# Two steps of six Fourier transforms in 64-by-64 parts of the matmul array

## The chip, the cores and the metric

The kernel runs on one core of a Trainium2 chip. The metric is the device time of one execution in microseconds. TensorE (PE) multiplies matrices into PSUM, VectorE (DVE) and ScalarE (ACT) work on SBUF and PSUM, GpSimd (POOL) on SBUF; SyncE (SP) and ACT issue most of the DMAs.

## The reference

Two blocks follow each other. The first filters each of the 8 sequences of 3008 tokens and 256 channels in the frequency domain; the second is a gated feed-forward layer on the 24064 tokens that result.

```python
def _attn_ref(x, filt_r, filt_i):                 # x: (8, 3008, 256), float32
    X = np.fft.rfft(x, axis=1)
    F = (filt_r + 1j * filt_i)[None, :, :]        # (1505, 256)
    Y = X * F
    y = np.fft.irfft(Y, n=x.shape[1], axis=1)
    return y.astype(np.float32)

def _moe_ref(x, w_gate, w_val, w_out):            # d_ff = 1536
    g = x @ w_gate
    silu = g * (1.0 / (1.0 + np.exp(-g)))
    val = x @ w_val
    return (silu * val @ w_out).astype(np.float32)
```

## The kernel before

All arithmetic is float32. One sequence is one transform b, 0 to 7. Its length is 47 x 64 (N1 = 47, N2 = 64, token = 64 n1 + n2), and it is done in four steps, each a set of matmuls against tables made on the host:

- First step, tiles pa. For each of the 64 values of n2, a 47-point transform over n1, of which the half spectrum of NS = 24 frequencies s is kept. For transforms 2 to 7 this is `stage1_paired` (L633): five values of n2 at a time (NP), 13 units; `pair` (L626) first makes, on DVE, the sums and differences of the rows n1 and 47 - n1 (L259 and L256), so that the real part comes from the sums (L639) and the imaginary part from the differences (L641). Two products of 256 columns per unit, one ACT copy (L645), one DMA from ACT's queue into the array d1 in DRAM. Transform 1 uses `stage1` (L658), transform 0 a form of its own before the main loop.
- Middle step there, tiles pb: `stage2a`, L698. For each s, the twiddle factors and the 64-point transform over n2 as one 128x128 table (64 complex points are 128 real rows), read from later_tbl. Two frequencies form a unit, 12 units. DVE then multiplies by the filter: the real part for all rows (L707), the imaginary part for the two halves of the partitions exchanged (L711, with the negation, and L714), and POOL adds (L256).
- Middle step back, tiles pc: `stage2b`, L731, the inverse over n2 for the same frequencies; ACT copies (L739), and the result goes to d2 in DRAM.
- Last step, tiles pd: `stage3`, L765, the inverse over s back to 47 values of n1, giving chunks y of 8 x 47 tokens (halved as TQ = 188 columns) with channels on partitions.

The feed-forward layer works on four chunks k of each transform and three groups g of the hidden width: 12 steps per transform, run by class Group. It multiplies polynomials of the blocks in a form that saves products: products P, Q (into banks wk), A, B (banks wa), E (banks we), all at L862, with sums on DVE, ACT and POOL between them; the projection W to the output (banks wA, wF, wG, L959) and its sums o (L256). While transform b is in its 12 steps, the pieces of transform b + 1 are woven in: the list `plan` says which piece belongs to which step, and each piece is a Python generator, of which every `yield` ends one stage.

The order is written out by hand. SCHEDULE (L88) is one step as a list of tokens; a token such as Q1, s13 or g12 names one operation of the group, a mark ' one of the group before, t1.2 the third stage of the second piece of the plan. `pin` keeps every engine's instructions in this order. There are no engine priorities: each engine takes its instructions in order and waits for what it needs.

Eight PSUM banks of 512 columns exist. Seven form the pool wps, which the products of the feed-forward layer share; one is the pool fps, which the pieces pa, pb, pc and pd of transforms 1 to 7 use in turn (`bank`, L620; fbank). The SBUF area lent (L213) holds the tables, inputs and outputs of the middle step. At marked tokens of each step SP issues the reload of the next group's weights wt_t (`reload_weights`, L405).

Of the kernel before, what the change touches and what calls it, by code (L numbers as in the profile page):

```python
# [41 lines left out]
FP32 = mybir.dt.float32  # L42
# [16 lines left out]
NH = 4  # L59
# [13 lines left out]
NP = 5  # L73
NPAIR = N1 // 2
N_PAIRED = -(-N2 // NP)

# [12 lines left out]
Q0 o3' z1.o' t4.2' W2 f0 S00' S01' i0 x0.o' t0.0 x1.o' i1 Q1 t0.1 x2.o' P3 i2 x3.o' f1 t4.3' W1 i3  # L89
x4.o' S10' x03 S11' i4 s13 x5.o' P1 i5 o1 t0.2 P0 o2 i6 z0.o c1 i7 D01 A13 g1 c0 i8 S20' Q2 S21' g0  # L90
y01 m13 t1.0 h0 i9 f2 s01 W6 t1.1 h1 i10 x23 D02 P2 o6 D12 A01 i11 c2 B13 g2 n3' m01 t0.3 S30' t1.2
x02 W7 S31' g13 y12 y02 B01 h13 o7 t1.3 t2.0 s02 s12 g01 h2 Q3 t2.1 h01 e12 A02 y23 W4 e02 y03 m02
g3 A12 o4 z2.o t2.2 E12 m12 B02 t2.3 l12 E02 u12 e13 g02 t3.0 h3 s23 l02 B12 v12 E13 t3.1 h02 u02
A23 n2 l13 g12 v02 W5 s03 e23 h12 e01 m23 A03 o5 z3.o u13 E23 t3.2 m03 v13 E01 l23 e03 t3.3 t4.0 l01
u23 B23 v23 u01 t4.1 E03 n1 v01 g23 B03 l03 W3 h23 g03 u03 h03 v03
# [6 lines left out]
""".split()  # L102
BLOCKS = (0, 1, 3, 2)
# [21 lines left out]
def dft_tables():  # L125
# [30 lines left out]

    paired = np.zeros((NP * (NPAIR + 1), 2, NP, NS))
    for j in range(NP):
        paired[NPAIR * j:NPAIR * (j + 1), :, j] = w[1:NPAIR + 1]
        paired[NP * NPAIR + j, 0, j] = 1.0  # L160
    paired = paired.reshape(NP * (NPAIR + 1), -1)


    pairs = np.arange(128).reshape(2, N2).T.ravel()
    later = np.stack([de[:, :, 0], de[:, :, 1][:, :, pairs]], 2)
    f32 = np.float32
    return (wf.reshape(NR, NK).astype(f32), wi.reshape(NK, NR).astype(f32),
            back.astype(f32), paired.astype(f32), np.ascontiguousarray(de).astype(f32),
# [4 lines left out]
def kernel(  # L173
# [11 lines left out]
    wf_host, wi_host, back_host, paired_host, de_host, later_host = dft_tables()  # L185
    wf_dram = nc.inline_tensor(wf_host, name="wf_tbl")
    wi_dram = nc.inline_tensor(wi_host, name="wi_tbl")
    paired_dram = nc.inline_tensor(paired_host, name="paired_tbl")
# [34 lines left out]

    def weights_of(b, k, g):
        return wt_1 if b == 0 and k < NT and g == 1 else wt_t
# [6 lines left out]
    w_dram = wdpool.tile([NG, 128, NPR, 2, 128], FP32, name="w_all")  # L232
    wo_t = cpool.tile([128, NJ, 7, 128], FP32)
# [19 lines left out]
    pin = tc.keep_in_program_order  # L253

# [229 lines left out]
    back_t, paired_t, differences, third = [], [], [], []  # L484

    def load_back():

        for n in range(3):
            t = rpool.tile([128, 2, 128], U32, name=f"paired_{n}", tag="pw", bufs=3)
            t = t.bitcast(FP32).rearrange("p b f -> p (b f)")  # L490
            (differences if n else paired_t).append(t[0:NP * (NPAIR + (not n))])
        t = rpool.tile([128, 2, 128, 2], U32, name="x_third", tag="raw", bufs=2)
        t = t.bitcast(FP32).rearrange("p b f two -> p (b f two)")
        third.append(t[0:NP * (NPAIR + 1)].rearrange("p (i c) -> p i c", c=C))
        pin(nc.sync.dma_start(out=paired_t[0][:, 0:2 * NP * NS], in_=paired_dram.ap()))
        t = rpool.tile([128, 2, 128, 2], U32, name="back", tag="raw", bufs=2)
        t = t.bitcast(FP32).rearrange("p b f two -> p (b f two)")
        back_t.append(t[:, 0:10 * N1])
        pin(nc.sync.dma_start(out=back_t[0], in_=back_dram.ap()))
# [15 lines left out]
    class Spectral:  # L515
# [25 lines left out]
        def load_x(self, u):  # L541
            if self.b == 0:
                rows = x[0].rearrange("(r n) c -> r n c", n=32)
                for a, n in ((0, 4), (4, 4)):
                    for r in (slice(0, 80), slice(80, NR)):
                        self.load(out=x0[u][r, a:a + n, :],
                                  in_=rows[r, 8 * u + a:8 * u + a + n, :])
            elif self.b > 1:
                if u < N_PAIRED:
                    t = third[0]  # L550
                    if u % 3 < 2:
                        t = xpool.tile([NP * (NPAIR + 1), 2, C], FP32, name=f"x_{self.b}_{u}",
                                       tag="x")
                    n2, pairs = min(NP * u, N2 - NP), NP * NPAIR
                    rows = x[self.b].rearrange("(n1 n2) c -> n2 n1 c", n2=N2)
                    back = bass.AP(tensor=x.tensor,
                                   offset=x.offset + ((self.b * N1 + N1 - 1) * N2 + n2) * C,
                                   ap=[[C, NP], [-N2 * C, NPAIR], [1, C]])
                    self.load(out=t[0:pairs, 0], in_=rows[n2:n2 + NP, 1:NPAIR + 1])
                    self.load(out=t[0:pairs, 1], in_=back)  # L560
                    self.load(out=t[pairs:pairs + NP, 0], in_=rows[n2:n2 + NP, 0])
                    self.x[u] = t
            elif u < N_ONE:
                self.x[u] = xpool.tile([NR, NV, C], FP32, name=f"x_{self.b}_{u}", tag="x")
                rows = x[self.b].rearrange("(r n) c -> r n c", n=32)

                for r in (slice(0, 80), slice(80, NR)):
                    self.load(out=self.x[u][r], in_=rows[r, ts(u, NV), :])

        def load_two(self, u):  # L570
            if u < N_TWO:
# [10 lines left out]
                if self.b < 2:  # L582
                    self.load(out=self.t2[u], in_=self.twos(self.d1, u))
                    return
                rows = self.d1.rearrange("a n c -> (a n) c").rearrange(
                    "(n s p) c -> p n s c", n=N2, p=2)
                for i in range(2):
                    self.load(out=self.t2[u][N2 * i:N2 * (i + 1)], in_=rows[i, :, ts(u, NV)])
# [37 lines left out]
        def pair(self, u):  # L626

            if u < N_PAIRED:
                a, b = [self.x[u][0:NP * NPAIR, i] for i in range(2)]
                pin(sub(nc.vector, differences[u % 2], a, b))  # L630
                pin(add(nc.vector, a, a, b))

        def stage1_paired(self, u):  # L633

            t1 = t1pool.tile([NP * NS, 2, C], FP32, name=f"t1_{self.b}_{u}", tag="t1", bufs=2)
            ps = self.bank(f"pa_{self.b}_{u}")[0:NP * NS]
            table = paired_t[0]
            m = NP * NS
            pin(nc.tensor.matmul(out=ps[:, 0], lhsT=table[:, 0:m], rhs=self.x.pop(u)[:, 0],  # L639
                                 start=True, stop=True))  # L640
            pin(nc.tensor.matmul(out=ps[:, 1], lhsT=table[0:NP * NPAIR, m:2 * m],  # L641
                                 rhs=differences[u % 2], start=True, stop=True))
            self.load_x(u + 3)
            yield
            pin(nc.scalar.copy(out=t1, in_=ps))  # L645
            n2 = min(NP * u, N2 - NP)

            rows = self.d1.rearrange("a n c -> (a n) c").rearrange("(r p) c -> r (p c)", p=2)
            pin(nc.scalar.dma_start(out=rows[NS * n2:NS * (n2 + NP)],
                                    in_=t1.rearrange("p i c -> p (i c)")))  # L650
            yield
            self.pair(u + 2)
# [449 lines left out]
    older = before = None  # L1102
    pieces_before = []
# [52 lines left out]
    for b in range(B):  # L1156
# [8 lines left out]
        if b:  # L1165
            one = [nxt.stage1_paired(u) for u in range(N_PAIRED)] if nxt else []
        else:
            one = [nxt.stage1(u) for u in range(N_ONE)]
        two = []
        for u in range(N_TWO + 2) if nxt else ():  # L1170
            two += [nxt.stage2b(u - 2)] if u > 1 else []
            two += [nxt.stage2a(u)] if u < N_TWO else []
        if nxt:
            plan[0] = one[0:2] + d[0][0:1] + one[2:3] + d[0][1:2]
            plan[1] = one[3:4] + d[0][2:3] + one[4:5] + d[0][3:4] + one[5:6]
            plan[2], plan[3] = (one[6:10], one[10:13]) if b else (one[6:11], one[11:16])
            plan[4] = d[1] + two[0:1]

            plan[5], plan[6] = [iter(())] + two[1:5], two[5:10]
            plan[7] = two[10:11] + d[2]  # L1180
            plan[8], plan[9] = two[11:16], two[16:21]
            plan[10], plan[11] = two[21:24], three(nxt, 0)
# [10 lines left out]
        for step in range(NCHUNK * NG + (b == B - 1)):  # L1193
# [16 lines left out]
            for place, token in enumerate(SCHEDULE):  # L1210
# [8 lines left out]
                elif op[0] == "t":  # L1219
                    n = int(op[1])  # L1220
                    ps = pieces_before if old else pieces
                    if n < len(ps):
                        next(ps[n], None)
                elif op[0] in "Wo" or op.endswith(".o"):
# [10 lines left out]
                if nxt and (step, op) == ((4, "P2") if b else (5, "A23")):  # L1235
                    nxt.load_two(0)
                if b + 2 < B and (step, op) in ((10, "Q2"), (10, "B01"), (11, "Q2")):

                    following.load_x(2 if step == 11 else int(op == "B01"))
                if b + 2 < B and step == 11 and op in ("A02", "B02"):  # L1240
                    following.pair(int(op == "B02"))
# [43 lines left out]
```

## Time and profile before

| what | value |
|---|---|
| three timed runs | 2888.11, 2889.03 and 2891.69 us, median 2889.03 us |
| profiled execution | 2891.35 us, of which the trace spans 2889.6 us |
| mean granted clock of TensorE | 0.998 of full speed |
| DMA | 558.89 MB, mean 193 GB/s |

The profile's page gives for each engine its busy time and the count of its instructions. PE is a matmul, PEld the load of its stationary operand, which overlaps the matmuls. In a group's row the columns are: line, engine, operation, output and inputs, shape, count, then the busy time and the mean of one in ns, then the idle time of the engine before it with what ended it. A float32 product of the program is two MATMUL rows and two LDWEIGHTS rows in the trace.

### The profile page before, as it was taken

How to read it: one execution, taken by the hardware profiler on the slowest of the kernel's cores; microseconds unless marked ns; L12 is line 12 of the kernel's file. 1: busy time of each engine (PE TensorE's matmuls, PEld its weight loads, DVE VectorE, ACT ScalarE, POOL GpSimd, SP SyncE). 2: the span in 40 equal slices, each digit the busy share in tenths (PEclk: the TensorE clock that was granted, in tenths of full speed). 3: DMA queues.
4: the chain of work that ended last, by engine and by line, in shares of the span. 5: the costliest groups of instructions: out<-in, count | busy, mean ns of one | idle time of the engine just before them, and what ended most of it. 6: DMA issues, size and time to landing. Idle time of an engine off the chain costs nothing.

```text
span 2889.6 us, 47316 instructions
## 1 busy us (share of the span) xinstructions
PE 2843.4 (98%) x14784; PEld 2434.3 (84%) x14784; DVE 2075.8 (72%) x4663; ACT 1576.1 (55%) x4190; POOL 1534.5 (53%) x1671
## 2 busy tenths in 40 slices
PE   7999999999999999999999999999999999999998
PEld 5777878888888888888888888888888888888887
DVE  6898767776767766777767677677677767766666
ACT  6775445555555455555555554555555555555554
POOL 4885665555445554446453555444554544555453
PEclk9999999999999999999999999999999999999999
DMA  8677865666566765667656566566665666645443
GB/s 227 218 265 245 278 209 176 181 219 196 182 190 180 229 185 184 197 182 216 196 183 197 179 208 205 177 195 184 209 193 189 185 205 195 206 142 161 147 137 82
DMA packets 396367, 558.89 MB, mean 193 GB/s; under 512 B 201079, under 2 KB 296585, under 8 KB 396117
## 3 DMA queue, kind: packets, MB, share of 16 engines
q1 hardware_dynamic: 366533, 506.80, 57.5%
q10 hardware_dynamic: 27792, 45.72, 4.7%
q0 software_dynamic: 1792, 3.34, 0.4%
q8 instruction: 120, 1.97, 0.3%
q14 instruction: 130, 1.06, 0.1%
HBM read 460.38 MB, written 95.34 MB: 192 GB/s over the span
## 4 chain that ended last, share of the span: by engine, by line
PE 87%; POOL 3%; issue 1%; DVE 1%; DMA 0%; ACT 0%; POOLq 0%; SPq 0%; DVEq 0%
PE wa L862 23%; PE wA L959 15%; PE wk L862 15%; PE we L862 12%; PE wG L959 8%; PE wF L959 3%; PE pd L765 3%; PE pc L731 2%; PE pb L698 2%; PE pa L639 1%; PE pa L641 1%; POOL out_dram L944 1%; POOL h L259 1%; DMA lent<-later_tbl 0%; DVE o L256 0%
## 5 line engine op out<-in xcount | busy, mean ns | idle before, releaser
L862 PE MATMUL wa<-y_t,wt_t 128*128 128x188 f32 x4464 | 879.1, 323 | 7.9 <-DMA y_t<-yt 1.7
L862 PEld LDWEIGHTS wa<-y_t,wt_t 128*128 128x128 f32 x4464 | 748.8, 190 | 89.3 <-ACT wa L888 11.3
L256 POOL TENSOR_TENSOR h<-h 128x376 f32<-128x376 f32 x190 | 184.9, 994 | 776.4 <-DVE h L909 776.4
L259 POOL TENSOR_TENSOR h<-h 128x376 f32<-128x376 f32 x572 | 565.5, 1010 | 15.4 <-DVE h L256 15.2
L862 PEld LDWEIGHTS wk<-y,wt_t 128*128 128x128 f32 x2976 | 500.9, 190 | 80.2 <-ACT f L877 0.8
L862 PE MATMUL wk<-y,wt_t 128*128 128x188 f32 x2976 | 565.1, 323 | 0.0
L959 PE MATMUL wA<-h,wo_t 128*128 128x376 f32 x1532 | 549.0, 481 | 3.5 <-DVE o L256 3.2
L862 PE MATMUL we<-y_t,wt_t 128*128 128x188 f32 x2232 | 431.7, 323 | 0.8 <-ACT we L893 0.7
L259 DVE TENSOR_TENSOR we<-we,m 128x376 f32<-128x376 f32 x576 | 316.4, 554 | 134.8 <-PE we L862 86.8
L959 PEld LDWEIGHTS wA<-h,wo_t 128*128 128x128 f32 x1532 | 279.2, 190 | 109.0 <-issue 3.5
L862 PEld LDWEIGHTS we<-y_t,wt_t 128*128 128x128 f32 x2232 | 369.4, 190 | 1.6 <-ACT we L893 0.9
L259 POOL TENSOR_TENSOR D<-f,f 128x376 f32<-128x376 f32 x288 | 280.5, 986 | 131.9 <-ACT f L877 123.2
L897 ACT COPY m<-wa 128x376 f32<-128x376 f32 x576 | 271.7, 472 | 86.0 <-PE wa L862 82.8
L263 DVE SCALAR_TENSOR_TENSOR y<-wk,c 128x376 f32<-128x376 f32 x480 | 243.1, 539 | 82.4 <-ACT we L893 53.9
L904 ACT ACTIVATE u<-we 128x188 f32<-128x188 f32 x576 | 188.8, 328 | 191.0 <-DVE we L259 170.9
L959 PE MATMUL wG<-h,wo_t 128*128 128x376 f32 x768 | 274.0, 479 | 0.0
L904 ACT ACTIVATE g<-wa 128x188 f32<-128x188 f32 x576 | 187.2, 326 | 157.2 <-PE wa L862 143.9
L877 ACT ACTIVATE f<-wk 128x376 f32<-128x376 f32 x288 | 139.1, 483 | 224.5 <-PE wk L862 153.8
L881 ACT COPY c<-wk 128x376 f32<-128x376 f32 x288 | 136.0, 472 | 215.7 <-PE wk L862 215.7
L884 DVE SCALAR_TENSOR_TENSOR x<-wk,f 128x376 f32<-128x376 f32 x192 | 104.1, 542 | 199.3 <-PE wk L862 196.9
L893 ACT COPY we<-y 128x376 f32<-128x376 f32 x480 | 220.8, 479 | 39.4 <-DVE h L909 24.7
L909 DVE TENSOR_TENSOR h<-wa,g 128x188 f32<-128x188 f32 x576 | 196.2, 345 | 31.5 <-ACT g L904 30.6
(157 smaller groups left out, 3857.8 us busy)
## 6 DMA issues: line engine op xcount, KB each, us to landing
wt_t<-w_all SPq DMA_DIRECT2D x174, 896.0 KB
wt_t<-w_all SPq DMA_DIRECT2D x174, 768.0 KB
lent<-later_tbl SPq DMA_DIRECT2D x84, 256.0 KB
lent<-in_filt_r_dram SPq DMA_DIRECT2D x336, 64.0 KB
d<-lent ACTq DMA_DIRECT2D x84, 256.0 KB
d<-t ACTq DMA_DIRECT2D x78, 240.0 KB
lent<-d SPq DMA_DIRECT2D x144, 128.0 KB
t<-d SPq DMA_DIRECT2D x112, 128.0 KB
```

What stands on the lines that cost most here:

```text
L256: return eng.tensor_tensor(out=dst, in0=a, in1=b, op=ALU.add)
L259: return eng.tensor_tensor(out=dst, in0=a, in1=b, op=ALU.subtract)
L263: return nc.vector.scalar_tensor_tensor(out=dst, in0=a, scalar=-1.0, in1=b, op0=ALU.mult, op1=ALU.subtract)
L862: pin(nc.tensor.matmul(out=ps[:, z], lhsT=self.wt[:, SLOT[p], z], rhs=rhs, start=start and z == 0, stop=True, skip_group_check=True))
L877: pin(act.mul(self.small(f"f{i}", f"f{i}", 1), t[f"k{i}"], -1.0))
L881: pin(act.copy(out=self.small(f"c{i}", f"c{i}", 1), in_=t[f"k{i}"]))
L884: pin(v.scalar_tensor_tensor(out=dst, in0=t[f"k{j}"], scalar=-1.0, in1=t[f"f{i}" if j == 3 else f"D{at}"], op0=ALU.mult, op1=ALU.add))
L893: pin(act.copy(out=self.bank(f"e{at}"), in_=t[f"y{at}"]))
L897: pin(act.copy(out=self.small(f"m{at}", "m", 4), in_=t[f"a{at}"]))
L904: pin(act.activation(out=self.small(op, "g", 3, 1)[:, 0], in_=ps[:, 1], func=AF.Silu))
L909: pin(v.tensor_tensor(out=dst, in0=ps[:, 0], in1=g, op=ALU.mult))
L959: pin(nc.tensor.matmul(out=self.tiles[at], lhsT=wo_t[:, JB * q + i, WO[p], :], rhs=self.hs[i][:, HID[p]], start=start and i == 0, stop=Tru ...
```

## The change

It concerns transforms 2 to 7 alone (b > 1).

- First step, new `quads`: tokens n2 and n2 + 32 lie on the two halves of the partitions, 47 rows each; the table is 64 columns wide (48 used). Eight pieces of four n2; a piece is four products of 512 columns, each on a 64x64 quarter of the array (row half by input half, column half by output half). The pairing of n1 on DVE is gone. Instead the sum and difference of the two halves of n2 (the first stage of the 64-point transform) are made from the banks: ACT copies one, DVE subtracts and adds the other.
- Middle step, new `fours`: four frequencies at a time, six groups. What is left of the 64-point transform is two 32-point transforms, each a 64x64 table: 8 products of 256 columns there and 8 back per group, again on the four quarters. One call holds the way back of group w - 1 and the way there of group w. On the way back the sum and difference of the halves are made from the banks as well.
- The product with the real filter is taken from the banks on DVE; ACT keeps a copy of the banks; four DMAs exchange its real and imaginary rows; DVE multiplies the exchanged copy by the imaginary filter, POOL adds.
- The filter is laid out once in DRAM (f_dram) during the first three steps of transform 1, its negated part by way of ACT.
- All products of one piece are issued together at the new token b0 (a burst), after W2 and before Q1; tokens b1 to b7 carry the remaining stages. Four bursts of `quads` fill steps 0 to 3 and seven of `fours` steps 4 to 10 of the transform before. The banks come from the pool wps, four per burst. stage2a and stage2b remain for transforms 0 and 1.

```diff
-Q0 o3' z1.o' t4.2' W2 f0 S00' S01' i0 x0.o' t0.0 x1.o' i1 Q1 t0.1 x2.o' P3 i2 x3.o' f1 t4.3' W1 i3
+Q0 o3' z1.o' t4.2' W2 b0 f0 S00' S01' i0 b1 b2 x0.o' t0.0 x1.o' i1 Q1 t0.1 x2.o' P3 i2 x3.o' f1
...
-        def pair(self, u):
...
-        def stage1_paired(self, u):
...
+        def quads(self, g):
+            pieces = (2 * g, 2 * g + 1)
...
+                for cp in range(2):
+                    for h in range(2):
+                        r = slice(64 * h, 64 * h + N1)
+                        pin(nc.tensor.matmul(
+                            out=banks[u, h][64 * cp:64 * cp + 64], lhsT=quad_t[0][r, 0:64],
+                            rhs=xt[r, 2 * cp:2 * cp + 2].rearrange("p n c -> p (n c)"),
+                            start=True, stop=True))
+            yield
...
+                pin(nc.scalar.copy(out=t1[u][:, :, 0], in_=low))
+                pin(sub(nc.vector, t1[u][:, :, 1], t1[u][:, :, 0], high))
+                pin(add(nc.vector, t1[u][:, :, 0], t1[u][:, :, 0], high))
...
+        def fours(self, w):
...
+                for s in (0, 2, 1, 3):
+                    for e in range(2):
+                        r = slice(64 * e, 64 * e + 64)
+                        pin(nc.tensor.matmul(
+                            out=home[e][s // 2 * 64:s // 2 * 64 + 64, s % 2 * C:s % 2 * C + C],
+                            lhsT=tb[r, 1, 64 * s:64 * s + 64], rhs=y[r, s],
+                            start=s % 2 == 0, stop=True, skip_group_check=True))
...
+                for s in range(2):
+                    for e in range(2):
+                        for p in range(2):
+                            r = slice(64 * p, 64 * p + 64)
+                            a = 64 * (2 * s + e)
+                            pin(nc.tensor.matmul(
+                                out=there[p][64 * e:64 * e + 64, ts(s, C)],
+                                lhsT=tb[r, 0, a:a + 64], rhs=t[r, s, e],
+                                start=s == 0, stop=True, skip_group_check=True))
+            yield
...
+                pin(nc.scalar.copy(out=t, in_=there[p]))
...
+                pin(nc.vector.tensor_tensor(out=y[:, a], in0=there[p], in1=self.f[w][:, 0, a],
+                                            op=ALU.mult))
...
+                    for r in range(2):
+                        self.load(out=pairs[0][:, r], in_=pairs[1][:, 1 - r])
...
+                    pin(nc.vector.tensor_tensor(out=q[:, a], in0=q[:, a], in1=self.f[w][:, 1, a],
+                                                op=ALU.mult))
+                    pin(add(nc.gpsimd, y[:, a], y[:, a], q[:, a]))
...
-        if b:
-            one = [nxt.stage1_paired(u) for u in range(N_PAIRED)] if nxt else []
...
+        bursts = [[] for _ in range(NCHUNK * NG)]
+        if b and nxt:
+            for n in range(N_QUAD // 2):
+                bursts[n] = nxt.quads(n)
+            for n in range(N_FOUR + 1):
+                bursts[N_QUAD // 2 + n] = nxt.fours(n)
```

## The prediction

> **What bounds the kernel now.** I read the busy times first, then the chain that ended last, then that chain in order of time, and only then the groups.
>
> ```profile
> PE 2843.4 (98%) x14784; PEld 2434.3 (84%) x14784; DVE 2075.8 (72%) x4663; ACT 1576.1 (55%) x4190; POOL 1534.5 (53%) x1671
> PE 87%; POOL 3%; issue 1%; DVE 1%; DMA 0%; ACT 0%; POOLq 0%; SPq 0%; DVEq 0%
> 1120.00:1480.00 360.00, 359.71 (x1880) 311.04 (x1879) 255.80 (x579) 192.95 (x514) 181.68 (x188) 1.00 0.64 195
> ```
>
> TensorE is busy throughout, and the chain is its own. A busy PE is not proof, since a matmul's row overlaps the next one's; the third line is a middle stretch of 360 us (columns: length, then busy time and count of PE, PEld, DVE, ACT, POOL, then clock, DMA share, GB/s), where PE lacks 0.29 us. The chain in order of time says it better:
>
> ```profile
> 1505.80 1.26 PE wF L959 x4
> 1507.06 0.43 PE pa L639 x2
> 1507.50 0.43 PE pa L641 x2
> 1507.93 1.28 PE wk L862 x8
> ```
>
> These are start, length and count. Each piece starts where the last ends, and no other engine stands between them. One product of the program is two MATMUL rows (two passes), and a pass costs its columns and nothing else: 1.26/4 = 0.315 us for 376, 1.28/8 = 0.160 for 188, 0.43/2 = 0.216 for 256 columns. So from about 100 us on, the time is the sum of the passes, and what the edit does to that sum it does to the time, as long as PE finds no new wait.
>
> **What the Trainium skill says.** "TensorEngine Tiling (Array Packing)", section Key Properties: parts of the array run independently, but changing the tiling mode drains the engine. "TensorE: Matmul & The Clock Gate", section Measured speedup vs the span model, gives 3.07 times for four parts side by side; its section The mechanism says that matmuls start and end strictly in program order. "PSUM — Partial Sum Buffer", section PSUM bank collisions raise a hardware error, says that parts on different rows may not write one bank together, and the edit does give each row half its own bank. No row of this trace uses less than the whole array, so none of the four is confirmed here.
>
> **The change part by part.** Removed, for transforms 2 to 7:
>
> ```profile
> L731 PE MATMUL pc<-lent 128*128 128x256 f32 x336 | 87.4, 383 | 4.4 <-DVE lent L714 3.5
> L698 PE MATMUL pb<-lent 128*128 128x256 f32 x336 | 86.3, 379 | 0.9 <-DMA lent<-d 0.9
> L641 PE MATMUL pa<-paired,paired 115*120 115x256 f32 x156 | 46.5, 378 | 0.0
> L639 PE MATMUL pa<-x,paired 120*120 120x256 f32 x108 | 32.2, 379 | 0.0
> L639 PE MATMUL pa<-x_third,paired 120*120 120x256 f32 x48 | 14.3, 379 | 0.0
> ```
>
> pb and pc serve seven transforms, of which transform 1 keeps its 48 passes each: 2 x 288 go. pa goes whole: 156 + 108 + 48 = 312. That is 888 passes of 256 columns at 0.216 = **191.8 us**.
>
> Added, per transform: 8 pieces x 4 products of 512 columns, and 6 groups of four frequencies x 16 products of 256 columns; two passes each. Over six transforms that is 384 passes of 512 columns (0.43 us alone, twice 0.216) and 1152 of 256: 165 + 249 = 414 us if they ran one by one. Everything hangs on how many run at once. Four at once: **103.5 us**. Two at once: 207. One at a time: 414.
>
> Overhead: the new products lie in 11 bursts per transform (4 + 7), 66 in all, each with a change of mode at both ends. The trace shows no such change. Below: nothing. Above: per change the tail of a pass and an unhidden weight load. A 188-column row lasts 323 ns and the next starts after 160, so the tail is 0.164; a LDWEIGHTS row lasts 0.190; 0.354 x 2 x 66 = 47 us. I take 0.25 per change, between the ends: 33 us. To that comes filling four parts one after another. The skill's matmul page, section LDWEIGHTS, prices a load by its columns, 107 ns for 128; L671 in this trace agrees: its 96-column passes follow each other after 3.55/32 = 0.111 us, the load's pace. 64 columns are then some 0.055 (estimate from that row). With both passes loaded in turn the fourth part starts 6 x 0.055 = 0.33 us late, of which I count 0.2: 13 us. Together **46 us**, range 15 to 60.
>
> Other engines, all beside PE. DVE loses, per transform, 13 pair sums and differences (36.6 + 31.5 + 27.9 + 17.6 over six = 18.9 us) and 36 products of 0.69 (24.8); it gains 16 half sums and differences and 36 operations of the middle step on 128x512, 52 x 0.69 = 35.9: 8 us less.
>
> ```profile
> L707 DVE TENSOR_TENSOR lent<-pb,lent 128x512 f32<-128x512 f32 x84 | 58.0, 691 | 51.8 <-PE pb L698 31.9 <-DMA wt_t<-w_all 16.5 <-DMA out_dram<-o 1.6
> L739 ACT COPY lent<-pc 128x512 f32<-128x512 f32 x84 | 49.1, 585 | 45.5 <-PE pc L731 45.4
> L256 POOL TENSOR_TENSOR lent<-lent 128x512 f32<-128x512 f32 x84 | 107.0, 1274 | 136.3 <-DVE lent L714 72.5 <-PE we L862 58.9 <-PE wk L862 3.7
> ```
>
> ACT has 26 copies of 0.585 in place of 25. POOL keeps 12 sums of 1.274. SP's issues fall from 2074 to 1720, ACT's rise from 191 to 209. Bytes rise from 556 to 583 MB, counted from the program; at a DMA share of 0.64 the extra 5% is hidden by the 29 us that one step leaves each load. The filter's copy in DRAM, with its negation on ACT, is made in the first three steps of transform 1 and read from the fourth on. The exchange of real and imaginary rows is four new DMAs per group on SP, behind two ACT copies. Behind them on SP wait the next group's loads and the reload of wt_t; by their places in the order the copies are issued some 4 us of a 29 us step earlier, and the exchange has 10 us before DVE reads it, so SP should not stand still.
>
> New waits on PE: a burst takes four of the seven wps banks, where pa, pb and pc had the fps bank for themselves. Following each bank in the program, its earlier user is released at least 2.1 us of PE work before the burst takes it, which is inside the spread of 1.3 to 6.5 us of before. The tightest is wA (W1) behind a burst: its bank is freed by a DVE sum that starts after an ACT copy, about 1.35 us after the burst, where PE arrives after 1.28. DVE has three operations of 0.69 (two half sums, one product) ahead of x03 and s13, which A13 needs: 2.1 + 2 x 0.55 = 3.2 us, against 3.8 us of PE work (Q1, P3, W1, P1, P0). It just fits. I allow 5 us in all (0 to 15).
>
> Sum against its own span: 2889.6 - 191.8 + 103.5 + 46 + 5 = 2852.3, a loss of 37 us. The three timed runs have a median of 2889.03 and the profiled execution 2891.35, so the span may stand for them; I forecast **2851 us**, own range 2816 (overhead 15, no waits) to 2872.
>
> **The rivals.**
> 1. **Only two parts at once.** The side that ends slower. In the built program the two passes of a product stand next to each other on the same part. If matmuls start strictly in program order, part B cannot start before part A's second pass, which waits for its first: two are in flight, never four. Then 2889.6 - 191.8 + 207 + 33 + 5 = 2943 us, range 2905 to 2965. For it: the page on order. Against it: the other page calls the parts independent, and its 3.07 is for four parts. It decides below 414/(191.8 - 51) = 2.9 passes at once.
> 2. **Four at once, but PE stands at the bursts.** The wA and s13 margins above are a few tenths. If each burst costs another 0.6 us of waiting, 40 us are given back: 2890 us, range 2872 to 2905. For it: before, PE waited for nothing. Against it: DVE, at 72%, has less to do.
> 3. **The parts run one by one.** 2889.6 - 191.8 + 414 + 33 = 3145 us. Nothing in the profile excludes it; only the skill speaks against it.
>
> **How the numbers follow.** Forecast 0.62, rival 1 0.25, rival 2 0.10, rival 3 0.03. About 0.2% (6 us) is what a measurement of this kernel can tell from no change. The range goes from 2812 to 2936: the forecast whole, rival 2 whole, and the nearer third of rival 1, 0.62 + 0.10 + 0.08 = 0.80. The forecast's own range is 2816 to 2872. Faster: 0.62 and half of rival 2, 0.66. Same: 0.04, from rival 2. Slower: 0.30.
>
> **What would show it.** Right: in a burst, rows of 64x64 parts that start about 0.054 us apart for 256 columns and 0.11 for 512 (four at once), and some 2.4 us from the row before a burst of the middle step to the row after. Rival 1: 0.11 and 0.21 apart. Rival 3: 0.216 and 0.43. Rival 2: an idle time ahead of wA or wa that a DVE release ended. The forecast is wrong if bursts last over 3.5 us in the mean, or if the DMA exchange holds up DVE in front of its product (L818 of the changed kernel).

## The result, and the profile after

The changed kernel takes 2840.43 us (median of four runs, 2836.95 to 2841.77), against 2890.0 us for the kernel before in four runs (2888.11 to 2891.69). The ratio is 0.983, with a 95% interval from 0.981 to 0.984: **49.6 us faster**. The profiled execution spans 2837.5 us, where that of before spans 2889.6 us; the accounts below are made against this difference of 52.1 us. The forecast was 2851 us.

The same two lines of the page as before, the busy times and the chain that ended last:

```profile
PE 2789.6 (98%) x15432; PEld 2315.4 (82%) x15432; DVE 2035.0 (72%) x4603; ACT 1567.1 (55%) x4202; POOL 1525.2 (54%) x1671
PE 85%; DVE 4%; POOL 3%; issue 2%; DMA 1%; ACT 1%; SPq 0%; ACTq 0%; DVEq 0%; POOLq 0%
```

PE has 648 more rows and 54 us less to do, since rows that run side by side are counted once. DVE's share of the chain has grown from 1% to 4%, and that is the first trace of a new wait. The middle stretch of 360 us, with the columns as before:

```profile
1120.00:1480.00 360.00, 359.31 (x2041) 299.03 (x2040) 256.94 (x590) 197.04 (x533) 185.47 (x193) 1.00 0.68 206
```

PE lacks 0.69 us instead of 0.29, so it is still the bound. But this column hides short stops, because a row's modelled end overlaps the next row's start. The stops show only in the distances between starts of successive rows, which is how everything below is counted. The chain around one burst of the first step (start, length, what):

```profile
1480.25 1.26 PE wF L1131 x4
1481.51 1.88 PE wqa L690 x16
1483.39 1.47 PE wk L1034 x8
1484.86 1.39 PE wA L1131 x4
1486.25 1.27 PE wk L1034 x8
```

Sixteen passes of 512 columns take 1.88 us. One after another they would take 16 x 0.43 = 6.9 us, and four at once 1.72. Next to the burst one sees what it costs its neighbours: the wk row after it takes 1.47 us where the undisturbed one at the end takes 1.27, and wA, behind that, 1.39 instead of 1.26. The longest bursts of the middle step look like this in the timeline of PE (start, length, engine, line, operation):

```profile
1282.73 0.80 PE L1131 MATMUL wF<-h,wo_t 128*128 128x376 f32 x2
1283.45 1.09 PE L749 MATMUL wqc<-lent 64*64 64x256 f32 x16
1284.37 1.04 PE L761 MATMUL wqb<-lent 64*64 64x256 f32 x16
1285.34 1.54 PE L1034 MATMUL wk<-y,wt_t 128*128 128x188 f32 x8
```

32 passes of 256 columns lie between 1283.45 and 1285.34. Inside, the single records show fours: four passes whose starts are 6 to 7 ns apart, then the next four 0.2165 us later (0.430 for 512 columns; the second four come 0.05 later than that), in all 66 bursts. The removed work has these rows in its place (groups, by shape):

```profile
L690 PE MATMUL wqa<-lent,quad 47*64 47x512 f32 x384 | 46.7, 602 | 0.0
L749 PE MATMUL wqc<-lent 64*64 64x256 f32 x576 | 39.4, 389 | 0.0
L761 PE MATMUL wqb<-lent 64*64 64x256 f32 x576 | 37.9, 378 | 0.0
```

The counts are those of the prediction, 384 and 1152. The busy times are unions of rows that overlap; by starts of rows the 66 bursts last 114.0 us: 24 of 1.878 (first step), 30 of 1.888 (way back and way there together) and 12 of 1.024.

**The account of the 52.1 us**, from the distances between starts:

| term | predicted | in the trace |
|---|---|---|
| passes removed | -191.8 | -191.8 |
| passes added, four at once | +103.5 | +103.5 |
| inside a burst, beyond that: 0.158 x 66 | in the 46 | +10.4 |
| last pass before a burst: 0.409 in place of 0.316, x 66 | in the 46 | +6.1 |
| first pass after it: 0.263 in place of 0.159, x 66 | in the 46 | +6.9 |
| new waits ahead of and inside wA | in the 5 | +7.8 |
| new waits ahead of and inside E13 (we) | in the 5 | +10.6 |
| waits of before around pc that are gone | not counted | -4.6 |
| sum | -37.3 | -51.1 |

The first two entries in the last column are the counts times the paces in the trace; the waits are counted from 400 us on. One microsecond is left unassigned. The overhead of a burst is thus 0.355 us, 23.4 us in all; the prediction took 46. The waits come to 13.8 net; it took 5. The experiments check these entries.

### The profile page after: what moved, and what is told of

Same layout as the page of the kernel before. It is cut to its first block, busy times and chain, and to the rows that moved or that the text cites. A ratio compares the mean times of both kernels' runs of the same rounds, so it can differ in the third digit from the quotient of the medians.

```text
span 2837.5 us, 48561 instructions
## 1 busy us (share of the span) xinstructions
PE 2789.6 (98%) x15432; PEld 2315.4 (82%) x15432; DVE 2035.0 (72%) x4603; ACT 1567.1 (55%) x4202; POOL 1525.2 (54%) x1671
## 2 busy tenths in 40 slices
DMA packets 363372, 586.58 MB, mean 207 GB/s; under 512 B 198388, under 2 KB 246260, under 8 KB 363024
## 4 chain that ended last, share of the span: by engine, by line
PE 85%; DVE 4%; POOL 3%; issue 2%; DMA 1%; ACT 1%; SPq 0%; ACTq 0%; DVEq 0%; POOLq 0%
PE wa L1034 22%; PE wk L1034 16%; PE wA L1131 15%; PE we L1034 12%; PE wG L1131 8%; PE wF L1131 4%; PE pd L937 3%; PE wqa L690 2%; PE wqc L749 1%; PE wqb L761 1%; POOL out_dram L1116 1%; DVE y L333 1%; DVE lent L818 1%; POOL h L329 1%; DVE o L326 0%
## 5 line engine op out<-in xcount | busy, mean ns | idle before, releaser
L1034 PEld LDWEIGHTS wk<-y,wt_t 128*128 128x128 f32 x2976 | 494.6, 190 | 106.7 <-issue 33.4
L1034 PE MATMUL wk<-y,wt_t 128*128 128x188 f32 x2976 | 571.3, 325 | 0.3 <-ACT f L1049 0.3
L329 POOL TENSOR_TENSOR h<-h 128x376 f32<-128x376 f32 x572 | 558.0, 998 | 15.4 <-DVE h L326 15.2
L326 POOL TENSOR_TENSOR h<-h 128x376 f32<-128x376 f32 x190 | 183.6, 988 | 707.0 <-DVE h L1081 696.7
L333 DVE SCALAR_TENSOR_TENSOR y<-wk,c 128x376 f32<-128x376 f32 x480 | 246.5, 540 | 58.7 <-ACT c L1053 36.0
L1081 DVE TENSOR_TENSOR h<-we,u 128x188 f32<-128x188 f32 x576 | 197.4, 344 | 29.8 <-ACT u L1076 19.0
```

The source lines that it names most:

```text
L326: return eng.tensor_tensor(out=dst, in0=a, in1=b, op=ALU.add)
L329: return eng.tensor_tensor(out=dst, in0=a, in1=b, op=ALU.subtract)
L333: return nc.vector.scalar_tensor_tensor(out=dst, in0=a, scalar=-1.0, in1=b, op0=ALU.mult, op1=ALU.subtract)
L1034: pin(nc.tensor.matmul(out=ps[:, z], lhsT=self.wt[:, SLOT[p], z], rhs=rhs, start=start and z == 0, stop=True, skip_group_check=True))
L1081: pin(v.tensor_tensor(out=dst, in0=ps[:, 0], in1=g, op=ALU.mult))
```

## The experiments

All ratios are to the kernel before on the same chip, which there had medians of 2889.88 to 2890.69 us.

### e1_grouped: order inside a burst

The products of a burst are issued so that two of the same part follow each other, four passes on one part in a row instead of two. The parts, banks and operands are the same.

```diff
-                for cp in range(2):
-                    for h in range(2):
+                xs[u] = xt
+            for cp in range(2):
+                for h in range(2):
+                    for u in pieces:
...
-                for s in (0, 2, 1, 3):
-                    for e in range(2):
+                for c, e in ((0, 0), (0, 1), (1, 0), (1, 1)):
+                    for s in (2 * c, 2 * c + 1):
...
-                for s in range(2):
-                    for e in range(2):
-                        for p in range(2):
+                for e in range(2):
+                    for p in range(2):
+                        for s in range(2):
```

> Products of a burst reordered so that two products of the same 64x64 part (four passes) stand next to each other, part after part; nothing else changes. Theory (each part takes its own passes, independently of the order of the program between parts): bursts keep their length, 1.88 us for quads and 1.89 for a double burst of fours, and the time stays at 2840 us within 4. Rival (starts in the order of the program, with the pattern of the changed kernel due to its order): one part runs its four passes before the next begins, bursts rise from 114 us in all to over 300, and the time is over 3030 us. Second rival (a look-ahead of few instructions): between the two, bursts of 2.5 us and more, over 2870 us.

It took 2855.14 us (2852.79 to 2856.57), ratio 0.988 (0.986 to 0.989). Its PE timeline at the same burst:

```profile
1293.26 1.11 PE L751 MATMUL wqc<-lent 64*64 64x256 f32 x16
1294.17 1.11 PE L763 MATMUL wqb<-lent 64*64 64x256 f32 x16
1295.21 1.54 PE L1036 MATMUL wk<-y,wt_t 128*128 128x188 f32 x8
```

The burst lasts 1.95 us in place of 1.89. With four passes of one part in a row the four parts still run together. Their starts are 13 to 14 ns apart instead of 6 to 7, about 3.3 ns for each pass in the program's order in both cases (an estimate from these starts; what sets it was not tested), and from the fifth or sixth round on one of the gaps is 57 ns. All bursts together grow by only 2.6 us. That disposes of the strict order on which the first rival rested. The expected time of 2840 was missed nevertheless, by 15 us, and the reason is for the most part a wait (columns: waiting engine and line, releaser, us in total, times, longest us):

```profile
PE wa L1036 <- DVE wa L1058: 5.9, 15, 1.0
PE wa L1036 <- POOL h L329: 4.0, 12, 0.3
```

By starts, the step from wk to wa now stands still 26 times, 13.3 us together; in the changed kernel three times. Twenty-four of these are 0.50 us each, one for each burst of the first step: the product A13 waits for s13, the DVE sum that fills its bank. Half of them stand under POOL, whose operation happened to end last, but in all 24 s13 ended 0.147 us before A13 started. In the grouped order the banks of the burst's first piece are released only near its end: ACT's first copy starts 2.01 us after the start of the burst (at 1491.43 us), where it is 1.14 us in the changed kernel (at 1481.44 us). DVE's half sums begin later, and s13, queued behind them, comes late. The prediction had put this margin at 3.2 against 3.8 us ("It just fits"): it fits with the order of the change, and not with this one.

### e8_double_one and e9_double_all: does the fullest part set the length?

In the first step's bursts the products of one part alone are issued twice (20 passes), or all of them (32). The diff is that of e8; in e9 the loop is `range(2)`. The added passes are extra work.

```diff
+                        for _ in range(1 if h or cp else 2):
                             pin(nc.tensor.matmul(
                                 out=banks[u, h][64 * cp:64 * cp + 64], lhsT=quad_t[0][r, 0:64],
```

> In the 24 bursts of quads, the products of one part (first row half, first column half) are issued twice, so 20 passes in place of 16 per burst; the result is the same. Theory (every part works off its own passes; a burst lasts as long as its fullest part): that part has 8 passes of 0.43 us in place of 4, burst 1.88 to 3.60 us, +41 us, 2876 to 2888 us, no less than with all parts doubled. Rival (the four parts share a throughput of four passes, whichever part they are for): 4 passes more cost 0.43 us per burst, +10 us, 2846 to 2856 us.

> The same with all products of quads issued twice, 32 passes per burst. Both theories: 8 rounds of 0.43 us in place of 4, burst 3.60 us, +41 us, 2876 to 2888 us. If the parts ran two at once or one at a time, it would be +83 or +165 us.

e8 took 2876.78 us (2875.11 to 2877.25), e9 2877.68 us (2876.71 to 2879.66), so 36 and 37 us more than the change, where 41 were expected. PE's timeline at a burst, of e8 and then of e9:

```profile
1152.21 1.43 PE L1132 MATMUL wF<-h,wo_t 128*128 128x376 f32 x4
1153.57 3.64 PE L691 MATMUL wqa<-lent,quad 47*64 47x512 f32 x20
1157.14 1.54 PE L1035 MATMUL wk<-y,wt_t 128*128 128x188 f32 x8
```

```profile
1151.73 1.43 PE L1132 MATMUL wF<-h,wo_t 128*128 128x376 f32 x4
1153.09 3.73 PE L691 MATMUL wqa<-lent,quad 47*64 47x512 f32 x32
1156.74 1.54 PE L1035 MATMUL wk<-y,wt_t 128*128 128x188 f32 x8
```

Four more passes on one part lengthen the burst from 1.88 to 3.57 us, sixteen more on all parts to 3.66. A pass on the fullest part costs its 0.43 us (4 x 0.43 = 1.72), and passes on the other three beside it cost next to nothing. So the passes are **independent between the parts, in sequence within one**, and a burst lasts as long as its fullest part. The other theory, in which added passes fill whatever slot is free, asked for some 10 us and is out. The times rise by less than the bursts, which grow by 40.7 and 42.7 us in all; a part of the difference is that behind these 24 longer bursts the wait ahead of wA is gone (30 late starts in place of 54).

### e2_split: the price of entering and leaving the mode

The bursts are cut in two: the token b0 stands ahead of W2 and again behind it, and the generators stop once more. 66 bursts become 120, with the same products.

```diff
-Q0 o3' z1.o' t4.2' W2 b0 f0 S00' S01' ...
+Q0 o3' z1.o' t4.2' b0 W2 b0 f0 S00' S01' ...
...
+                if u == pieces[1]:
+                    yield
```

> Each burst cut in two, with the four passes of W2 between the halves: 120 bursts in place of 66 (24 of quads and 30 double ones of fours are cut, 12 single ones are not), the same products. Theory (a change of mode costs a fixed 0.35 us per burst: 0.09 before, 0.16 in it, 0.10 after): +54 x 0.35 = +19 us, less up to 5 us of the wait before wA, whose bank is then freed earlier: 2852 to 2861 us. Rival (the overhead is filling and emptying of the long burst, not the change): the cost follows the products and stays, 2836 to 2844 us.

It took 2850.98 us (2848.77 to 2851.56), ratio 0.986 (0.985 to 0.988), 10.6 us more than the change. PE's timeline at a first-step burst:

```profile
1172.71 0.80 PE L1037 MATMUL wk<-y,wt_t 128*128 128x188 f32 x4
1173.44 1.09 PE L692 MATMUL wqa<-lent,quad 47*64 47x512 f32 x8
1174.46 1.53 PE L1134 MATMUL wF<-h,wo_t 128*128 128x376 f32 x4
1175.92 1.09 PE L692 MATMUL wqa<-lent,quad 47*64 47x512 f32 x8
1176.94 1.54 PE L1037 MATMUL wk<-y,wt_t 128*128 128x188 f32 x8
```

From 1173.44 to 1174.46 are 1.02 us for eight passes, 0.86 and again 0.16: the 0.16 is paid per burst, not per pass. By starts, entries cost 5.0 us more, the bursts 8.7, exits 5.5, together 19.2 us for 54 more bursts, or 0.356 us each. That is the 0.355 of the account by another way. The waits at wA are gone here (7.8 us, where up to 5 were expected to go), as only half of a burst's banks are then left to be emptied late; 19.2 - 7.8 = 11.4 against 12.3 in the spans. The time lies 1 us under the expected interval.

### e3_later: the product that holds up E13

Two tokens are moved later in the order: b6, the second of the two products of a group with the imaginary filter (L818) with POOL's sum of it, and b7, the load of the next group's filter.

```diff
-A02 y23 b6 W4 e02 y03 ... t2.3 l12 b7 E02 u12 e13 ...
-l02 B12 v12 E13 t3.1 h02 u02 A23 n2 l13 g12 ...
+A02 y23 W4 e02 y03 ... t2.3 l12 E02 u12 e13 ...
+l02 B12 v12 E13 t3.1 h02 u02 b6 A23 n2 l13 b7 g12 ...
```

> Token b6 (second product with the exchanged copy on DVE and its sum on POOL) moved from before W4 to behind u02, and b7 (load of the next filter) behind l13. Theory (the product of two SBUF operands, 0.96 us in place of 0.69, delays e13 on DVE, and E13 on PE waits for it): the idle time of PE between wa and we goes, 10 us less, 2828 to 2834 us. Rival (e13 is late for another reason, such as the wait for c1 or the transposition): the idle time stays, 2838 to 2843 us. Second rival (the later sum or filter load is late for the next burst): over 2845 us.

It took 2830.99 us (2827.56 to 2832.41), ratio 0.979 (0.978 to 0.981), 9.4 us less than the change. In the trace of the changed kernel, the product E13 starts late 12 times, twice per transform, by 0.508 us each, and its next pass by another 0.104; three more times it is late in a less regular way. In the twelve its releaser is e13 (L333), the DVE sum that fills its bank, queued behind b6. PE's waits list it so, with less time, since they count from the modelled end of the row before:

```profile
PE we L1034 <- DVE we L333: 4.1, 12, 0.3
```

With b6 behind E13 these twelve are gone. Two irregular ones remain, at 507 and 535 us, where transform 1 passes into 2 (4.5 us here, 2.2 in the changed kernel). The spans differ by 7.0 us, of which 5.2 lie behind the start of the first burst.

Why b6 takes long enough to matter shows in the groups. L818 of the changed kernel and then L779, the product with the real filter of the same shape:

```profile
L818 DVE TENSOR_TENSOR lent<-lent 128x512 f32<-128x512 f32 x72 | 69.1, 960 | 0.0
L779 DVE TENSOR_TENSOR lent<-wqb,lent 128x512 f32<-128x512 f32 x72 | 49.1, 682 | 14.4 <-DMA out_dram<-o 9.6 <-ACT raw L775 4.8
```

L818 of e3:

```profile
L818 DVE TENSOR_TENSOR lent<-lent 128x512 f32<-128x512 f32 x72 | 53.6, 745 | 0.0
```

The prediction had 0.69 us for both kinds. L779 reads one operand from a bank; L818 reads both from SBUF. The timeline of the changed kernel, all engines, shows one pair of L818:

```profile
1296.50 0.68 DVE L818 TENSOR_TENSOR lent<-lent 128x512 f32<-128x512 f32 x1
...
1297.32 1.27 POOL L326 TENSOR_TENSOR lent<-lent 128x512 f32<-128x512 f32 x1 [2.04 <-PE wa L1034]
1297.37 0.54 DVE L333 SCALAR_TENSOR_TENSOR y<-wk,c 128x376 f32<-128x376 f32 x1
1297.82 1.32 DVE L818 TENSOR_TENSOR lent<-lent 128x512 f32<-128x512 f32 x1
```

The first product takes 0.68 us. POOL's sum of its result follows (the last to release it was, by this profile, a product of PE), and the second product, which starts while that sum runs, takes 1.32. DVE's sum L333 between them, with a bank among its operands, runs in its usual 0.54 while POOL is at work. Over the whole trace, 36 of the 72 products start while a POOL sum or difference runs, and their mean is 1238 ns; the other 36 have a mean of 681 ns and none is above 683. In e3, 12 start under one (1070 ns), 60 do not (680 ns). The Trainium skill, "SBUF — State Buffer", section Who interferes with whom, says that a DVE instruction with two SBUF inputs contends with a GpSimd instruction that reads SBUF, and that one with at most one does not. The trace agrees, and gives the price: 0.56 us in the mean. It also shows the form: all 36 lengthened products end 545 to 552 ns after the end of the POOL operation that ran when they started, however much of it was left, and so do the 12 of e3. That is how it looks when the product stands until POOL's operation is over, and not when both run on at a slower pace.

In each of the twelve steps with a late E13 both products are lengthened, the first to 1.05 to 1.08 us and the second to 1.31, and DVE has an output to transpose (L1102, 0.58 us) between b6 and e13:

```profile
1324.19 1.06 DVE L818 TENSOR_TENSOR lent<-lent 128x512 f32<-128x512 f32 x1
1325.89 1.31 DVE L818 TENSOR_TENSOR lent<-lent 128x512 f32<-128x512 f32 x1
1328.15 0.58 DVE L1102 STREAM_TRANSPOSE o<-o 128x384 f32<-128x384 f32 x1
1329.09 0.55 DVE L333 SCALAR_TENSOR_TENSOR we<-wk,c 128x376 f32<-128x376 f32 x1
```

In twelve other steps only the second is lengthened, and nothing is transposed; there E13 is in time, but for one step, where that product took 1.60 us in place of 1.31 and E13 came 0.23 late. So the lengthening can decide it: without the 0.63 us at the second product e13 would be in time for E13 (an estimate from these figures). No run took the lengthening away and left the product in its place, and the transposition has its share.

### e6_real_from_copy: both operands from SBUF, where it was one

The other half of the same cause: the product with the real filter reads ACT's copy in SBUF instead of the bank.

```diff
-                pin(nc.vector.tensor_tensor(out=y[:, a], in0=there[p], in1=self.f[w][:, 0, a],
+                pin(nc.vector.tensor_tensor(out=y[:, a], in0=raw[p], in1=self.f[w][:, 0, a],
```

> One part of the change alone undone: the product with the real filter reads ACT's copy in SBUF in place of the bank. Theory (a DVE operation with two SBUF operands stands against POOL's, as the other product does with 0.96 us, one with a bank operand does not): the product's mean rises from 0.68 to between 0.75 and 0.96 us, DVE is 5 to 20 us busier, and as s13 sits behind it PE waits somewhat more: 2841 to 2850 us. Rival (the duration depends on the size alone): 0.68 us, 2837 to 2842 us.

Its row in the groups:

```profile
L779 DVE TENSOR_TENSOR lent<-raw,lent 128x512 f32<-128x512 f32 x72 | 73.6, 1023 | 14.4 <-DMA out_dram<-o 14.4
```

From 682 to 1023 ns, with nothing changed but where one operand lies. In both kernels 66 of the 72 overlap work of POOL: with the bank they take 681 ns, with the copy 1053; the six that overlap nothing take 691 and 693. The lengthening is shown, then, and is more than the 0.75 to 0.96 us expected. But the time is 2840.7 us (2839.64 to 2842.95), that of the change and of the rival. DVE's 22 us more (2057.2 busy) lie where no matmul waits. POOL's busy time rises too, by 20.6 us to 1545.8. What the change gains by taking this product from the banks is DVE time, and none of the device time.

### e7_pool_product: L818 on POOL

```diff
-                    pin(nc.vector.tensor_tensor(out=q[:, a], in0=q[:, a], in1=self.f[w][:, 1, a],
+                    pin(nc.gpsimd.tensor_tensor(out=q[:, a], in0=q[:, a], in1=self.f[w][:, 1, a],
```

> The product of the exchanged copy with the imaginary filter on POOL in place of DVE; places in the order as in the changed kernel. Theory (that product's time on DVE delays e13): DVE loses 69 us, POOL gains 72 x 1.27 = 91 us, the idle time between wa and we goes, 2828 to 2834 us. Rival (POOL, in order, now carries 2.5 us in one piece ahead of the differences D and the sums that A and W wait for): new idle time at those, over 2842 us.

```profile
L818 POOL TENSOR_TENSOR lent<-lent 128x512 f32<-128x512 f32 x72 | 92.1, 1280 | 0.9 <-PE wA L1131 0.9
```

It took 2832.41 us (2830.98 to 2834.87), ratio 0.980 (0.978 to 0.981), 8.0 us less than the change; the two kernels' runs don't overlap, though the ends of the two ratios' intervals do. A slower engine (1.28 us a product) is the better place, because E13 does not wait for POOL. The twelve waits of 0.508 us are gone, as in e3, by another edit. So it is L818 ahead of e13 on DVE that costs them. From the start of the first burst on, this span is 7.2 us shorter than that of the change.

### e4_swap: another product behind the burst

To test the wait ahead of wA, W1 and P1 change places, so that the bank of W1 has longer to come free.

```diff
-t4.3' W1 i3 x4.o' ... s13 b3 x5.o' P1 i5 ...
+t4.3' P1 i3 x4.o' ... s13 b3 x5.o' W1 i5 ...
```

> Tokens W1 and P1 exchange places, so that PE has 0.64 us more work between a burst and the first product into the bank wA. Theory (wA waits for the burst's bank, freed by DVE's sum): the 0.06 to 0.08 us of idle time before wA and the 0.075 inside it go for quads and shrink for fours, 3 to 8 us less, 2832 to 2838 us. Rival (the wait is for something else or moves to o1 on DVE, which then has no P1 in front): 2839 to 2845 us.

It took 2858.8 us (2856.35 to 2861.9), ratio 0.989 (0.988 to 0.991): 18 us slower than the change. PE's timeline behind a burst:

```profile
1179.98 1.95 PE L690 MATMUL wqa<-lent,quad 47*64 47x512 f32 x16
1181.85 2.44 PE L1034 MATMUL wk<-y,wt_t 128*128 128x188 f32 x12
1184.13 1.43 PE L1131 MATMUL wA<-h,wo_t 128*128 128x376 f32 x4
```

The wait ahead of wA is gone, as was meant: its 109 late starts (7.8 us) are one here. But the twelve wk passes take 2.28 us from start to start, where twelve undisturbed ones take 1.91 and the exit adds 0.10. Stops between wk passes sum to 28.7 us, in 208 places from 400 to 2500 us, against 6.4 in the changed kernel (which are the exits). P1 adds into the bank k1, and must wait until ACT has read k1 for f1, a dependence that the expectation had left out. The time of this run therefore says nothing on the wait; only the vanished stops do. The next one is clean.

### e5_early: e3, and the burst ahead of W2

```diff
-Q0 o3' z1.o' t4.2' W2 b0 f0 S00' S01' ...
+Q0 o3' z1.o' t4.2' b0 W2 f0 S00' S01' ...
```

and the edit of e3.

> The kernel of e3_later, and in addition the burst (token b0) before W2 in place of behind it, so that PE has 1.27 us more work between the burst and the first product into wA. Theory (the wait before and in wA, 7.8 us in all, is for DVE's sum out of the burst's bank): that idle time goes, 2821 to 2826 us. Rival (the burst now asks for its banks 1.27 us sooner and stands for them; the third bank's last reader lies only 1.5 us of PE work ahead): idle time in front of the burst in place of it, 2829 to 2845 us.

It took 2821.42 us (2820.35 to 2823.45), ratio 0.976 (0.975 to 0.978): **68.5 us less than before, 19 less than the change**, the fastest of all. The burst now has W2's four passes behind it, 1.36 us more in which DVE frees the bank. The stretch of 360 us:

```profile
1120.00:1480.00 360.00, 360.00 (x2057) 300.80 (x2056) 259.29 (x593) 199.27 (x532) 190.06 (x198) 1.00 0.70 210
```

and PE's timeline at a burst:

```profile
1160.27 0.80 PE L1034 MATMUL wk<-y,wt_t 128*128 128x188 f32 x4
1161.00 1.95 PE L690 MATMUL wqa<-lent,quad 47*64 47x512 f32 x16
1162.88 1.53 PE L1131 MATMUL wF<-h,wo_t 128*128 128x376 f32 x4
1164.24 1.44 PE L1034 MATMUL wk<-y,wt_t 128*128 128x188 f32 x8
1165.52 1.43 PE L1131 MATMUL wA<-h,wo_t 128*128 128x376 f32 x4
```

wA follows wk after 1.28 us, its eight passes and nothing more. The waits at wA are out (7.8 us), and so are the twelve at E13; three irregular ones of E13 remain (0.48, 1.90 and 1.36 us, between 476 and 535 us), so that of its 10.6 us 6.6 are gone. The span falls from 2837.5 to 2819.0, by 18.5 us, but 4.5 of these lie ahead of the first burst, where no edit acts and two executions simply differ. The 13.9 us behind it stand against 7.8 + 6.6 = 14.4. The mode itself costs what it did: the pass ahead of the burst is late by 93 ns, the one behind it by 104.

## Why the prediction was right, and where not

**The passes removed and added.** Right: 888 passes of 0.216 us went, and the new ones run four at once at the expected pace, 0.054 us per pass for 256 columns and 0.11 for 512 in the mean. Their starts come in fours rather than evenly, which the prediction had not pictured.

**Rival 1, only two at once** (chance 0.25): wrong. It rested on the built program, where the two passes of a product stand next to each other on one part, and on the Trainium skill, "TensorE: Matmul & The Clock Gate", section The mechanism, by which matmuls start strictly in program order. Here the measurement decides otherwise between parts: of the four products of a piece in the first step (parts A to D), C and D complete a bank, and only their second passes carry a semaphore. In program order these would be the sixth and eighth pass; in the records they are the seventh and eighth, in all 24 bursts. So the first four rows are first passes: B's starts 6 to 7 ns behind A's and some 0.47 us ahead of A's second. The grouped order (e1) says the same. Within one part the order stands (e8). The section's span, one matmul and about 4 ns for each further part, is near what is seen. "TensorEngine Tiling (Array Packing)", section Key Properties, independent parts and a drain at each change of mode, is confirmed on the first count. On the second the trace shows a price, 0.355 us for a burst's two changes; that it is a drain is not shown, as the first pass of a burst starts 0.07 us before the modelled end of the pass ahead of it.

**Rival 3, one by one**: out by the same rows.

**The overhead, 46 us.** The mechanism was right, its size twice too large: 23.4 us. Two terms of the sum failed. The 33 us for changes of mode took 0.25 at each end, between nothing and the whole of a pass's tail and an unhidden weight load (0.354); the entry costs 0.093, the exit 0.104, and 0.158 lies within the burst, mostly behind its last round. The 13 us for filling the parts one after another are wrong in kind: the weight loads of the four parts start 5 to 8 ns apart, not 0.055 us, so the parts fill side by side.

**The waits, 5 us.** Here the result was worse, 18.4 us of new waits, less 4.6 of old ones. Of the two places, wA was named as the tightest, with 1.35 against 1.28 us, and gave just that 0.07 us ahead of it in 54 bursts; the 0.08 within it was not foreseen. The s13 margin held. The other place, E13, was not seen: the step that failed is the one that priced DVE's 36 middle-step operations all at 0.69, and followed DVE's queue only as far as s13. For L818 the price holds only where POOL is not at work on SBUF at the time; it took 0.96 in the mean, and 1.24 where POOL was.

**Rival 2, PE stands at the bursts** (0.10): the mechanism is there at 0.15 us a burst instead of 0.6.

**What was costed at nothing** stayed so. DVE has 41 us less to do, against some 47 from the working. DMA moves 586.58 MB, against 583, and L818 waits 0.0 us for the exchange; a hold-up there was one of the two marks of a wrong forecast. The other was bursts over 3.5 us in the mean; they take 114.0/66 = 1.73.

So the forecast came out close, 11 us above the time, in part by luck, with errors of both signs: 22.6 us too much for the mode, 8.8 too little for waits net of those removed. In spans that is 13.8 of the 14.8 us between the sum, 2852.3, and the trace, 2837.5; the rest is the microsecond left unassigned. The upper end of its own range, 2872, is also 4 us below what its largest overhead and largest waits add up to (2876).

What stays open is why PE's four-at-once starts get a gap of 57 ns late in a grouped burst, and what the irregular waits of 1.4 to 4.4 us at 535 to 539 us, where transform 1 passes into 2, depend on. Neither was tried, nor was why ACT's copies are released so late in that order.

## What to carry to other kernels

When small products are packed onto parts of the array, count the passes of the fullest part and a fixed price per burst (0.36 us here), and then put the burst where the engines that empty its banks have slack: a burst finishes four banks at once, and the waits on DVE that came with the bursts cost nearly as much here (18.4 us) as entering and leaving the mode (23.4). A DVE operation with two SBUF operands should be priced by what POOL does at that moment; moving it behind the operation that PE waits for, or to POOL, gained 9.4 and 8.0 us here. A busy column near 100% does not show stops of a tenth of a microsecond; distances between starts of rows do.

## What the hardware showed that was not expected

- Passes of different parts overtake each other: with two passes of one part in a row, and with four, all four parts run together; the starts within a round are 6 to 7 and 13 to 14 ns apart.
- Weight loads of the four parts run side by side, their starts 5 to 8 ns apart.
- Two mode changes cost 0.355 us per burst: 0.093 ahead of it, 0.158 in it, 0.104 behind it; within 3 ns the same for bursts of 8, 16 or 32 passes, while two passes of one part follow each other (with four, 32 passes have 0.22 in them).
- A DVE product of two SBUF operands, 128x512 float32, takes 681 ns alone and 1238 in the mean when it starts while POOL adds from SBUF; with one operand in a bank it takes 681 ns beside POOL, too. The lengthened product ends 545 to 552 ns after POOL's operation, whatever was left of that at its start (78 cases in three runs).
